# Block-masked attention and a feed-forward layer: the first product of scores takes 128 rows instead of 68

## The chip, the cores and the metric

The kernel runs on one core of a Trainium2 chip. The metric is the time of one execution on the device, in microseconds (us). The core has five engines with queues of their own: PE (TensorE, the matrix unit), DVE (VectorE), ACT (ScalarE), POOL (GpSimd) and SP (SyncE, which here issues every DMA transfer). A matmul is two instructions on PE: a load of the stationary operand (LDWEIGHTS, shown as the lane PEld) and the MATMUL itself, which streams the moving operand past it.

## The reference

Eight batches of eight heads, 576 positions, 64 numbers per head; q, k and v are random. Each position sees its own block of 64 positions and all blocks before it. What comes out of the attention, 4608 rows of 512, goes through two matrices with a nonlinearity between them.

```python
scores = scale * np.matmul(q, k.transpose(0, 1, 3, 2))
mask = block_i >= block_j                     # blocks of 64 positions
scores = np.where(mask, scores, -1000000000.0)
scores = scores - np.max(scores, axis=-1, keepdims=True)
attn = np.exp(scores)
attn = attn / (np.sum(attn, axis=-1, keepdims=True) + 1e-09)
out = np.matmul(attn, v)
...
h = x @ w_in                                  # 4608x512 @ 512x2048
g = np.where(h >= 1, h, np.where(h <= -1, 0.0, (h + 1) ** 2 / 4))
return g @ w_out                              # 4608x2048 @ 2048x512
```

## The kernel before

**Two streams of work share the engines.** The attention goes pair by pair (two heads at a time; 8 batches of 4 pairs). The feed-forward layer goes by chunks of 512 rows and 128 hidden columns: `ffn_in` (L806, twelve matmuls of 512 columns) and `ffn_out` (L830 and L835, twelve more). Both are written as generators of steps and interleaved; the feed-forward layer follows the attention at a distance of one chunk.

**Numbers in two parts.** Most matmuls read the 32-bit type fp32r, which keeps fewer digits; so an operand is split in a high part and a low part (the rounding error of the high part), and a product is the sum of high by high, high by low and low by high.

**The scores.** In batches 0 and 1 the scores are plain 32-bit products of 64 rows (L555), and the mask is added by a small product of the tile `hide` (L563). `hide` is 128 rows by 2 by 64 columns; it is zero but for its rows 0 and 64. From batch 2 on (`far` and `raw` pairs) the method `product` makes them by two matmuls that accumulate in one bank `ps_s`:

- L531 multiplies `qa` and `ka`. Rows 0 to 63 of these tiles hold the high parts of q and k, one row for each of the 64 numbers of a head; rows 64 to 67 hold four rows of a mask (`mrow`), put there once at the start by the DMAs of L251 and L252. So the matmul takes KA = 64 + 4 = 68 rows. Rows 68 to 127 of both tiles are neither written nor read.
- L532 multiplies `qb` and `kb`, 128 rows, which carry high by low and low by high at once.

A pair has two heads and four tiles of 128 queries each, with 128, 256, 384 and 512 keys: eight such products a pair, 24 pairs, 192 in all. The last 64 queries of both heads go another way (`scores_last`, L609 and L612). Then come the softmax (DVE and ACT), a round trip by DMA that turns the weights into fp32r (`prr<-pr`), their transposes on PE (L636) and the product with v (L687). For each later pair, the DMAs of L477 copy the high parts from `qb` and `kb` into rows 0 to 63 of `qa` and `ka`.

**The order on each engine is fixed.** After all instructions are emitted, the tables `QUEUES` (one for each engine, compressed) tell in which order they stand in that engine's queue. They were made for one list of instructions: a kernel that emits other instructions needs other tables. PE, DVE and ACT take their queue strictly in turn, and so does SP, which issues the DMAs. The landings of SP's DMAs are counted by eight semaphores in rotation (they are named DMAHW0 to DMAHW7); before a DMA is issued, the one eight places ahead of it must have landed.

**Names on the way:** `qn`, `kn` and `en` are q, k and their last blocks as loaded for batches 0 and 1; `qk` holds them transposed; `bits` is a piece of a weight matrix that is being split, `ws` and `wo_split` the split pieces of w_out on chip and in memory, `wo` a piece loaded again; `xl` and `spare` take the round trip of the weights in batch 1.

Of the kernel before, what the change touches and what calls it, by code (L numbers as in the profile page):

```python
# [11 lines left out]
F32 = mybir.dt.float32  # L12
# [61 lines left out]

QUEUES = {
    "PE": (
        'c-rk&S#ld85CsNik!)F3BrA(ksY)d|g%9D|<OVrIZkL}NB)tL6Ald#;zgM$}VW9i*nvruoybEq{k?x1miY*DwgS6o<M+ZM0R'
        'A1*NdKNqCS@ad>L@dBQ9_+JmmoUJ4L1qqW{5+m>e}Q`-<Bz)qP88oY==|GQ*HQV4PqH4ds8jXR*uwFf?q+GZrq-_}uGG!;Q{'
        'H|H>IgahD63c3?^&+1yAk4wj>14>JOOK5BedjR+83=iUW#mx^MN?ZtaU8L{t6#}N9l7<JQZ!<0jokYa8sUf)R;jk>eiJ#LL{'
        's{9{1$Yh5R;Av}2P6wq>27dxY~RBIAAGdbO)Z+xf@F&9x0HVoQ;1;J_70QVYHItXvSD$a#)(otnDJvm~X8_GR_$wo!8Is+LE'  # L80
        '(qbzRSj;d}4zxQ;9?6G!zC^}4(ftUTri=H19tF|v=fhcw>jXh;N!ZC~gaz)e~?~<$M5@U_}K<?x`7Fw5CRnZK(RpJV6XfK**'
        '_3nTNc+bmQxy~jUEqk-yb*9cW{SKCKLq3o64vsTW-_P*tQAYki)J{cB&#&mZo)6zjqFy3pQ>pD<{k2EieYDm+#~!G%0y#f(Q'
        '10O~kL2MQW)(?Sj*%75xlJ@y{(@A_LLMcnp6EJ~BXVm{UjzTDPC@#&wOke9>|&XnJrc_Mv58X8>?KoQGUl9J(KM?yHa^sjoX'
        'OQuc9Oa~4aMuYnhQCJxu|cpm-#%^KJyYzUDflxrN7|l_^;ynFYcS{NgTsj{CIY61AYmxE`PxJJGJm0)PHaB{{)VX89X#m_WL'
        'QXUQoMcD!L<&z<j@JRwYVbWTLsWat4FJU@#aA27|$1Fc=I5gTY`h7z_r3!C){L3<kshf`9Kz7zY'
    ),
    "DVE": (
        'c-rk$+fKtU3_VGjrfV5!0>m3a3<UrGg*cv@#7SEO4@_e7QKC8*AKy}7gaK$c1Prh^Nz@(95qCWA(c^}ON$3fIzXmz)=%y13m'
        'aWY8z$`mPCwg4jvz0@-4bmo>M`U>-lycw|Lv|k72E?Kl&b)Hs$hHR>fxjLY*;DYjxN^@vfa4Av7n0R@|5mh#c8(mA#S8B~^I'
        '0qQf-t=@mc)v8?=-*BII1|1;)vQOo&6xR;t8duWv<4={-UY|B&t})o@?vnR?pDh+T>HG?36MxG`C}WyFznVmUeH}W8d5oI$<'  # L90
        'A+elb{=iMvVL>{WD55LZU29ID-Xy05;GGByxg1r(VApFk7)QZ7sdT>-ChKWD@hwcpA};Fr^Kq3Alz7vFcs{Tx#5w;0-vIr(X'
        'eSX#FEweBd6A+1Ed?4fCHXtq%8X*N^rS!K~krRx53%H!qS)H60S*;RGV@nMy#y>HUL)hym}$#X9`%>Ns07n?ofi{8UVboJ?O'
        'p?i(We_KVr61(|Ehx~O>Fs;kExpd9`S8Ugs{haS_qq{t|>wCMtx68@n?|9BFUxp_LiU'
    ),
    "Activation": (
        'c-rk!?Q+8)46{r~((a?()^&UTC!H~lgURx*cfIZgmjoP3mIXvagUm7#Edw$K*|SGynj}_p6CE^Xv~1Shi~c|A`z+5yuf}!M@'
# [6 lines left out]
        'c-muNzzrC&@EPH3Mg}G*%>tyE!E6?&8i*<;6xA@j$SN4I+Qx`s^GF8(GI#(c'  # L103
    ),
    "SP": (
        'c-rk#yKWRg5Uifv+uhr{UEdw}d3X4Y2oXXA{sbffzQK;{%&{L55kf)&$&zydLWCSy;sXdsAs`|k;UfsBuAMu91=s-+iKn&mt'
        'gi0rnN5+RB}-8PXv1h3EkS`d+6U)}W(m)a5paZ>sDdY5yhG02oaSC8Y)MQH9U_dFjAtG81;<*<Eq*<IhBX|rZxeL`=k&{kS|'
        'sWP<9Tdg4m0#~#0(ASqhcQv9m+eAd9*+?oZ&=%vovts!9eJ~vaXd?o3o6)XOk<VK&~L(H0Eg0+qt~u%-TIG`DW5wipBF@mDV'
        'isO%NtFh-+PAG0ncBo;=pSC7wcfkK#K)c(1}8>1x!KteQuf=<wYI+>W&ly00N_#q3l0xb?*p$lH_J5%;<gRq$-U3J2ES*ZX7'
        'u=J6aKv^KowxW{oeY5^lSTc!B{v+_!uVvF3lPF}_sH<kG}BD+yT73*nI+QXRrmQ|6tz(@A?Y=ul`%GZdP)7z@$H}N0f3%<)I'  # L110
        'U_(0(xVUeR*_ZgllOcA^SUvD|64hx{_iW1SE0*w#pXto>#!au-$Gev34Lr1wZqV;<lQl`OZD~{j91`WL&sKBo3O8Blw-ywss'
        'l311NA^@@EBT&YnNOeCj;&)^Oy0(N#g5%z6tL1=Dl~p$GJ;x$T)j4%-azA*#vAfK<X7|k6&Vz#QSm#^`3rW@GoN}kkta-lk3'
        'Et>dH*@~zxBM<d#(5X>J5?iGDN`7EydN^RdG%G0gmoAg8'
    ),
}

# [7 lines left out]
def block_attn_then_ffn(  # L124
# [232 lines left out]
    class Pair:  # L357
# [27 lines left out]
        def load_qk(self):
            if not self.raw:
                self.load("q")
                self.load("k")
# [4 lines left out]
            for i, src in enumerate(copies):
                for j in range(2):
                    head = src[self.b, 2 * self.hp + j]
                    nc.sync.dma_start(
                        self.qk[:, j * NTL : (j + 1) * NTL, i, :].bitcast(F32),
                        head[:SM].rearrange("(p t) d -> p t d", t=NTL),  # L400
                    )
# [126 lines left out]
            self.pb = att1.tile([P, 2, NTL, G1], F32, tag=f"pb{turn}", name=f"pb{turn}")  # L528

        def product(self, ps, j, c0, n):  # L530
            nc.tensor.matmul(ps, qa[:KA, j, c0 : c0 + P], ka[:KA, j, :n], start=True, stop=False)  # L531
            nc.tensor.matmul(ps, qb[:, j, c0 : c0 + P], kb[:, j, :n], start=False, stop=True)  # L532

        def inverse(self, total):
# [399 lines left out]
```

## Time and profile before

| | |
|---|---|
| time before, median of 3 runs | 1170.87 us (1169.71 to 1171.76) |
| the profiled execution's own time | 1173.48 us |
| its span, first to last instruction | 1171.4 us |
| mean granted clock of TensorE | 0.996 |
| PE busy | 1140.3 us, 97% of the span |
| DVE, ACT, POOL busy | 716.0, 623.7, 268.3 us |
| mean busy share of the DMA queue's transfers | 61.2% of 16 engines |

How to read the rows. A group's row has the line, the engine, the operation, `out<-in`, the number of rows and columns of the stationary operand in use (`68*128`), the shape of the moving operand, the count, the busy time in us with the mean duration of one in ns, and the idle time ahead of them. Matmuls overlap: one of 512 columns is shown with 389 to 400 ns although a new one starts each 0.23 us, so a sum of durations is not time. A row of the timeline has the start, the time it took, the engine and the instruction. PEld and PE are two lanes of the same engine.

### The profile page before, as it was taken

How to read it: one execution, taken by the hardware profiler on the slowest of the kernel's cores; microseconds unless marked ns; L12 is line 12 of the kernel's file. 1: busy time of each engine (PE TensorE's matmuls, PEld its weight loads, DVE VectorE, ACT ScalarE, POOL GpSimd, SP SyncE). 2: the span in 40 equal slices, each digit the busy share in tenths (PEclk: the TensorE clock that was granted, in tenths of full speed). 3: DMA queues.
4: the chain of work that ended last, by engine and by line, in shares of the span. 5: the costliest groups of instructions: out<-in, count | busy, mean ns of one | idle time of the engine just before them, and what ended most of it. 6: DMA issues, size and time to landing. Idle time of an engine off the chain costs nothing.

```text
span 1171.4 us, 19270 instructions
## 1 busy us (share of the span) xinstructions
PE 1140.3 (97%) x6384; PEld 905.8 (77%) x6384; DVE 716.0 (61%) x1858; ACT 623.7 (53%) x1531; POOL 268.3 (23%) x215
## 2 busy tenths in 40 slices
PE   7889998999999999999999999999999999999998
PEld 4556666778888888888888888888888888888886
DVE  7887887666666666666666666666666663222222
ACT  6887766455555555555555555555555553222222
POOL 3443555111121121111111111111111112222222
PEclk9999999999999999999999999999999999999999
DMA  6778777687887876665556565665566443423423
GB/s 190 226 231 245 261 231 235 189 240 235 246 263 237 256 230 187 174 202 180 169 163 212 177 177 172 201 187 173 165 206 196 132 146 98 140 90 96 138 90 108
DMA packets 195649, 219.54 MB, mean 187 GB/s; under 512 B 131280, under 2 KB 145616, under 8 KB 194784
## 3 DMA queue, kind: packets, MB, share of 16 engines
q1 hardware_dynamic: 195552, 218.33, 61.2%
q8 instruction: 51, 0.84, 0.3%
q14 instruction: 46, 0.38, 0.1%
HBM read 135.79 MB, written 31.98 MB: 143 GB/s over the span
## 4 chain that ended last, share of the span: by engine, by line
PE 83%; DVE 1%; DMA 1%; ACT 0%; issue 0%; POOL 0%; SPq 0%; ACTq 0%
PE ph L806 32%; PE po L830 21%; PE po L835 10%; PE ps_av L687 6%; PE ps_t L636 4%; PE ps_s L531 4%; PE ps_s L532 3%; PE ps_qk L469 1%; PE ps_s L609 1%; PE ps_s L612 1%; DMA wo<-wo_split 0%; DMA qn<-in_q_dram 0%; DVE t L816 0%; DVE t L819 0%; PE ps_s L555 0%
## 5 line engine op out<-in xcount | busy, mean ns | idle before, releaser
L821 POOL TENSOR_TENSOR gl<-t,gh 128x512 fp32r<-128x512 f32 x144 | 188.9, 1312 | 804.1 <-ACT gh L820 700.9
L830 PE MATMUL po<-wo,gh 128*128 128x512 f32 x1152 | 304.0, 397 | 0.9 <-DMA wo<-wo_split 0.5
L830 PEld LDWEIGHTS po<-wo,gh 128*128 128x128 f32 x1152 | 212.9, 189 | 45.5 <-ACT ps_s L583 0.7
L806 PE MATMUL ph<-xh,wih 128*128 128x512 f32 x576 | 230.1, 400 | 2.1 <-DVE t L819 2.1
L806 PE MATMUL ph<-xh,wil 128*128 128x512 f32 x576 | 227.2, 394 | 0.0
L806 PE MATMUL ph<-xl,wih 128*128 128x512 f32 x576 | 226.2, 393 | 0.0
L816 DVE SCALAR_TENSOR_TENSOR t<-t 128x512 f32<-128x512 f32 x144 | 101.5, 705 | 189.6 <-ACT t L815 189.5
L815 ACT ACTIVATE t<-ph 128x512 f32<-128x512 f32 x144 | 86.2, 599 | 176.0 <-PE ph L806 175.8
L835 PE MATMUL po<-wo,gl 128*128 128x512 f32 x576 | 164.0, 393 | 0.2 <-POOL gl L821 0.2
L820 ACT CAST gh<-t 128x512 fp32r<-128x512 f32 x144 | 89.3, 620 | 111.5 <-DVE t L819 111.4
L583 ACT ACTIVATE pr<-ps_s,nm 128x128 f32<-128x128 f32 x192 | 100.4, 525 | 82.7 <-DVE nm L578 68.5
L578 DVE TENSOR_REDUCE nm<-ps_s 128x1 f32<-128x384 f32 (+3 forms) x256 | 121.4, 485 | 25.6 <-PE ps_s L532 12.6
L835 PEld LDWEIGHTS po<-wo,gl 128*128 128x128 f32 x576 | 108.3, 188 | 23.6 <-POOL gl L821 0.6
L806 PEld LDWEIGHTS ph<-xh,wih 128*128 128x128 f32 x576 | 108.3, 188 | 23.2 <-DVE t L819 2.6
L806 PEld LDWEIGHTS ph<-xh,wil 128*128 128x128 f32 x576 | 108.2, 188 | 23.0
L806 PEld LDWEIGHTS ph<-xl,wih 128*128 128x128 f32 x576 | 108.4, 188 | 19.3 <-DVE xl L697 0.2
L819 DVE TENSOR_TENSOR t<-ph,t 128x512 f32<-128x512 f32 x144 | 98.8, 686 | 2.3
L636 PEld LDWEIGHTS ps_t<-ident_r,prr 128*128 128x128 f32 x600 | 68.6, 139 | 21.5 <-issue 0.4
L537 DVE TENSOR_SCALAR sm<-sm 128x1 f32<-128x1 f32 x256 | 37.2, 151 | 77.1 <-ACT pr L583 69.2
L651 ACT COPY pb<-ps_t 128x512 f32<-128x512 f32 (+1 forms) x128 | 68.0, 532 | 10.3 <-PE ps_t L636 8.3
L589 DVE TENSOR_SCALAR pr<-pr,sm 128x128 f32<-128x128 f32 (+2 forms) x192 | 70.0, 385 | 4.6 <-DVE sm L538 0.3
L636 PE MATMUL ps_t<-ident_r,prr 128*128 128x128 f32 x600 | 70.7, 236 | 0.0
(95 smaller groups left out, 1442.9 us busy)
## 6 DMA issues: line engine op xcount, KB each, us to landing
wo<-wo_split SPq DMA_DIRECT2D x144, 512.0 KB, 3.6
prr<-pr SPq DMA_DIRECT2D x96, 192.0 KB, 2.7
prr<-pr SPq DMA_DIRECT2D x48, 256.0 KB, 2.6
out_dram<-ob SPq DMA_DIRECT2D x36, 256.0 KB, 3.7
bits<-in_moe_w_in_dram SPq DMA_DIRECT2D x16, 512.0 KB, 4.4
vs<-in_v_dram SPq DMA_DIRECT2D x64, 128.0 KB, 3.5
bits<-in_moe_w_out_dram SPq DMA_DIRECT2D x16, 512.0 KB, 4.0
wo_split<-ws SPq DMA_DIRECT2D x16, 512.0 KB, 3.2
```

What stands on the lines that cost most here:

```text
L578: nc.vector.tensor_reduce(out=nm[:, i : i + 1], in_=ps[:, cs], axis=AX.X, op=ALU.max, negate=True)
L583: nc.scalar.activation(raw[:, cs], ps[:, cs], AF.Exp, bias=nm[:, i : i + 1], scale=1.0, accum_out=sm[:, i : i + 1],)
L636: nc.tensor.transpose(out.bitcast(F32R), src, ident_r)
L687: nc.tensor.matmul(ps[j * D : (j + 1) * D, lo_col:], self.vs[j][:, kt, :], x, start=i == 0, stop=i == len(heads[0]) - 1,)
L806: nc.tensor.matmul(ph, w[:, cc, fs], x[:, cc, xs], start=(cc == 0 and i == 0), stop=(cc == NCC - 1 and i == 2),)
L815: nc.scalar.activation(t_, ph, AF.Relu, bias=0.5, scale=0.5)
L816: nc.vector.scalar_tensor_tensor(out=t_, in0=t_, scalar=1.0, in1=t_, op0=ALU.min, op1=ALU.mult)
L819: nc.vector.tensor_tensor(out=t_, in0=ph, in1=t_, op=ALU.max)
L820: nc.scalar.copy(gh, t_)
L821: nc.gpsimd.tensor_tensor(out=gl, in0=t_, in1=gh.bitcast(F32), op=ALU.subtract)
L830: nc.tensor.matmul(po[tt], gh[:, ts_], wo[:, w, :], start=(fc == 0 and w == 0), stop=False)
L835: nc.tensor.matmul(po[tt], gl[:, ts_], wo[:, 0, :], start=False, stop=fc == NFC - 1)
```

## The change

Three things are done.

- The first matmul of `product` takes all 128 rows of `qa` and `ka`, not the first 68.
- So that rows 68 to 127 add nothing, a new method `clear_below` fills them with zeros, once, by two DMAs (one for `qa`, one for `ka`; 60 rows of 8 pieces of 512 bytes, 240 KB each). They read `hide`, whose rows 4 to 63 are zero, and they read the same 128 columns eight times. They are emitted when q and k of the first pair of batch 2 are fetched.
- The tables of PE, DVE and SP are new, since two more instructions are emitted.

```diff
 QUEUES = {
     "PE": (
-        'c-rk&S#ld85CsNik!)F3BrA(ksY)d|g%9D|<OVrIZkL}NB)tL6Ald#;zgM$}VW9i*nvruoybEq{k?x1miY*DwgS6o<M+ZM0R'
...
+        'c-rk&+i}}45IleYNlBJ$E0UFmGnvUGslr9Ln{<#G(p`R1NbZFfLD~M#?G8y11cAH79w>kw4m=DHs(S*p$T9GJfQaX)eTLjFn'
...
         def fetch(self):
             if self.raw:
+                if (self.b, self.hp) == (RAW, 0):
+                    self.clear_below()
                 for dst, src in zip(copies, (q, k)):
...
+        def clear_below(self):
+
+            part, _, cols = hide[KA - D : D, :, :].ap
+            zeros = bass.AP(
+                tensor=hide.tensor, offset=hide[KA - D : D, :, :].offset,
+                ap=[part, [0, 2 * SM // P], [1, P]],
+            )
+            for t_ in (qa, ka):
+                nc.sync.dma_start(
+                    t_[KA:].bitcast(F32).rearrange("p j (n c) -> p (j n) c", c=P), zeros
+                )
...
         def product(self, ps, j, c0, n):
-            nc.tensor.matmul(ps, qa[:KA, j, c0 : c0 + P], ka[:KA, j, :n], start=True, stop=False)
+            nc.tensor.matmul(ps, qa[:, j, c0 : c0 + P], ka[:, j, :n], start=True, stop=False)
             nc.tensor.matmul(ps, qb[:, j, c0 : c0 + P], kb[:, j, :n], start=False, stop=True)
```

The new lines push later ones down: L531 becomes L545, L555 becomes L569, L563 becomes L577, L823 becomes L837.

The first place is on SP, in the work of batch 1, where the two new DMAs stand. Names ahead of the bracket are as above; in the bracket are the semaphores that the row waits for (the numbers behind the underscore say nothing). Before:

```order
L436 DMA kn<-in_k_dram 128x4x64 [waits DMAHW4_49,PE_49]
L823 DMA wo<-wo_split 128x1024 [waits DMAHW6_49,DMAHW5_49,PE_49]
L347 DMA xl<-pr 128x384 [waits DVE_49]
L315 DMA wo_split<-ws 128x1024 [waits DMAHW7_49,Pool_49]
L436 DMA qn<-in_q_dram 128x4x64 [waits DMAHW0_49]
L347 DMA xl<-pr 128x384 [waits DMAHW1_49,DVE_49]
L266 DMA bits<-in_moe_w_in_dram 128x1024 [waits DMAHW2_49]
L436 DMA qn<-in_q_dram 128x4x64 [waits DMAHW3_49]
L315 DMA wo_split<-ws 128x1024 [waits DMAHW4_49,Pool_49]
L347 DMA xl<-pr 128x384 [waits DMAHW5_49,DVE_49]
```

and now:

```order
L450 DMA kn<-in_k_dram 128x4x64 [waits DMAHW4_49,PE_49]
L395 DMA qa<-hide 60x8x128 [waits DMAHW5_49]
L395 DMA ka<-hide 60x8x128 [waits DMAHW6_49]
L837 DMA wo<-wo_split 128x1024 [waits DMAHW7_49,PE_49]
L347 DMA xl<-pr 128x384 [waits DMAHW0_49,DVE_49]
L315 DMA wo_split<-ws 128x1024 [waits DMAHW1_49,Pool_49]
L450 DMA qn<-in_q_dram 128x4x64 [waits DMAHW2_49]
L347 DMA xl<-pr 128x384 [waits DMAHW3_49,DVE_49]
L266 DMA bits<-in_moe_w_in_dram 128x1024 [waits DMAHW4_49]
L450 DMA qn<-in_q_dram 128x4x64 [waits DMAHW5_49]
L315 DMA wo_split<-ws 128x1024 [waits DMAHW6_49,Pool_49]
L347 DMA xl<-pr 128x384 [waits DMAHW7_49,DVE_49]
```

The two stand behind `kn` and ahead of `wo`. The eight rows behind them each wait for another landing than before; from the last row shown on, every row waits for the same transfer as before (the last `xl` waits for this `wo` in both). No other row of SP moved, and nothing else on it was added.

The second place is on PE, in the first pair of batch 0, where plain scores (of `qk`) and their mask (of `hide`) are made. Before:

```order
L555 MATMUL ps_s<-qk_145 64x64
L555 MATMUL ps_s<-qk_145 64x128
L563 MATMUL ps_s<-hide 64x64 x2
L555 MATMUL ps_s<-qk_145 64x192
L555 MATMUL ps_s<-qk_145 64x256
L563 MATMUL ps_s<-hide 64x64
```

and now:

```order
L569 MATMUL ps_s<-qk_145 64x64
L569 MATMUL ps_s<-qk_145 64x128
L577 MATMUL ps_s<-hide 64x64
L569 MATMUL ps_s<-qk_145 64x192
L577 MATMUL ps_s<-hide 64x64
L569 MATMUL ps_s<-qk_145 64x256
L577 MATMUL ps_s<-hide 64x64
```

One small matmul of the mask stands one row later. Seventeen rows of PE moved in this manner, all in batches 0 and 1 and nearly all of L563, by one place or two. From batch 2 on, the rows of PE stand as they stood, and no product of scores waits for a semaphore that it did not wait for before.

The third place is on DVE, at the start of the program, where `hide` is filled and the first q and k are taken out of `ps_qk`. Before, two fills of `hide` stood ahead of the copy into `qk`:

```order
L512 TENSOR_SCALAR qc_108<-ps_qk 64x64 x2
L248 MEMSET hide 1x64 x2
L513 COPY qk_145<-ps_qk 128x64
L273 TENSOR_SCALAR bits<-bits 128x512
L578 TENSOR_REDUCE nm<-ps_s 128x1 x2
```

and now they stand behind it:

```order
L526 TENSOR_SCALAR qc_108<-ps_qk 64x64 x2
L527 COPY qk_145<-ps_qk 128x64
L248 MEMSET hide 1x64 x2
L273 TENSOR_SCALAR bits<-bits 128x512
L592 TENSOR_REDUCE nm<-ps_s 128x1 x2
```

Two other small fills of DVE moved by a place. ACT and POOL stand as before.

More of the change, by code (lines that the diff above doesn't have):

```diff
@@ L76 @@
     "PE": (
-        'c-rk&S#ld85CsNik!)F3BrA(ksY)d|g%9D|<OVrIZkL}NB)tL6Ald#;zgM$}VW9i*nvruoybEq{k?x1miY*DwgS6o<M+ZM0R'
[L78 to L85, printed above, removed]
+        'c-rk&+i}}45IleYNlBJ$E0UFmGnvUGslr9Ln{<#G(p`R1NbZFfLD~M#?G8y11cAH79w>kw4m=DHs(S*p$T9GJfQaX)eTLjFn'
@@ new lines @@
+        'D|-f2#ZnE)#<T8_VLh@Ev#X{SUq0l2;Jxaf01`c!5`QoCywtLmib@n<utPOxMYM-wY2vDJ3M~#uUT8Jsr73S*D|)B`u1B;Mo'
+        '7_zyn0^yJnMCa8zrsisPw8i;R%`Iiueq2ui6)_H(rV?^*%C3owbZ5xVyp!<VpM7GtXJucgUj9jNImD5;bKIv!lz(o-h(opN@'
+        'O>=!VsrIOeg*g4&W!0Uq)Ei79xWxm@ky(RTi^st%~ys3LY8iRWxQM(%kfdhOHd3eW63;9RGsuF|T;N|oA|#kadg$+4?i8R?d'
+        'z-ot^b?tu4uy#w}Ci>2#*)?wld9OpzWqUXnoMcbFL!PyThy99YRVkT0z$%o_!`L*WiImcL{KC(L{kFqwYie}WUkXCTZd(p(J'
+        'cZ)pYdoHi2)Y-(NC2#h-&eXX^DiT(z?uLCH_#GN&;J%;n?omhnz^t80nqFSfbvYls6;-{+%0^XmSW$oJQCN8*ex%qvSC&V0x'
@@ L86 @@
+        '0yrb9y!ZM4xdq0fpwL=PZUqNO+411SrpDn86~M6`8u*AQme1N2JTgzy!LNvxhNvpg*>}>#OL=z6J<TK(@b5?SaOD}X;N!!d{'
+        '{ejW>*K@Ny_e2z7DjS8+MX#Q+>0Y&gZ!Hg=;u>RWJKi{RJn-e^u9ifp5AeNembD;|1OZ`VvrG{=oBhZrL;Y?=AhGpwTIVhbG'
+        'E?Kb6(<)vg({?!*%^{XR6S60|Qd>h4~YGZ+j8gTY`h7z_r3!C){L3<iV2U@#aA27|$1Fc|(9`~#@R7wr'
     ),
     "DVE": (
-        'c-rk$+fKtU3_VGjrfV5!0>m3a3<UrGg*cv@#7SEO4@_e7QKC8*AKy}7gaK$c1Prh^Nz@(95qCWA(c^}ON$3fIzXmz)=%y13m'
-        'aWY8z$`mPCwg4jvz0@-4bmo>M`U>-lycw|Lv|k72E?Kl&b)Hs$hHR>fxjLY*;DYjxN^@vfa4Av7n0R@|5mh#c8(mA#S8B~^I'
@@ L90 @@
[L90 to L93, printed above, removed]
+        'c-rk$+fKtU3_VHOrWdwp0>m3a3<UrGg*cv@#7SEO4@_e7QQA5eAKy}7gaK$c46x{MmY@e%`Z~}s*wNY@4HMB3Jb(3Ze}h>pT'
@@ new lines @@
+        'd`3OECZtvJ<ROb%27@S=`hiAM3N^$E=Qg*Wap7>KrFVxnP$!$$#ze}^Vb6-c?#YaX71SsaNM5bLbMvr??szv<-{>ryzuHX@3'
+        'msj3)3rONvwGHPR}<QClv=`96|e}y&r^HT0*XAaq^znUli4VL>21Tacx^U)iJcUHu}^kJGqPu&F$FUkZBIfQm@T==$k#E5%w'
+        '|b7lU<~xSO=iPDSSgVP=%dp;%43yW$%$V?DtYK$a=+4pgx(<-!!u6=+rN=Zv_l_FEb8d~<3pWL>BE!u@WzpM9+T7DL@JXFqK'
+        'gOU*Xl)`8;a<4oX79-8WeX7k0GDgH)j%_@sVDpmHMQywqprhH;ElTA_g6dzW(>hmW4Tg~Dr7d>w!hv|Q#?P9ZM+N}4m5nZ{v'
+        'S?FG)@?Tf6U5VX%qeK3>$e7mU(p<V`|0}jz&3?}Jx6xf6+wH#H?%Va`@pn9zmM_1J2#x'
@@ L105 @@
     "SP": (
[L106 to L113, printed above, removed]
+        'c-rk#yKWRg5Uifv+uhsSUEdw}0e1&}B8Lbe0)GOM1AhZVkP(A;L<orh0>}x7EktC=u>+?jAR=($k8nVB?c5109uAO5JguE)b'
+        '#+(IY>E^eS&9-s7e>oy2@33LADkzeB|LwQfM;lkDtJ<1A31k(ntPeBB{6;Uh%jO@p7q!l92+rr`1Sc2R`Ha5m#9nFqhBu66{'
+        '6lUp2r3jFh@T}%+Y`WYW6|Vp}Z5BM+-E=XS|c&JPlm;Fcf;AtQ%$3<t$_G+2qP7kSmBcjX7HM2A1euDVv;`yLT=BOu9=kdG0'
+        'IHn?=qk!o&#it!XS~3TkS~;~jLwQwZ--d?yI+mDrTFR$<A?d8DZp-(A9uSnr@a8{t}1kjlqxAf`axz7&tSS4C98vmvV-Sbtw'
+        'XA_K69*ErPLaKP~)$N8uQjNojw=8u_`SK>Xk$erutO^k6_nV%3@MGZCY2jX$1eN5PISsj@R9I?M;%Vhebe2s_&y{|@oQ~x2p'
+        ';Z!~W>)N@)#ckVRU*Zc-MtESx>VdbDs7@=oYg1;&xQbW&OlPKdZhFZ+-n2yT;I55zgMNP-tVx1<mPRGO6QX?e)f%o{;RY+cY'
+        'eA9P%KOXRwwEef$v5@EeEP!f+ZwKm$=gIP*|F=40#>@BLgP0fBdBG>)km}04YYn~ydnQfem37<mO*h^6~FRaJY#1)^O<KGdC'
+        'K(X*kc)#_wQr>Th9x<7kdA%-Vk~Jh6wnvr8r+ZFRpFh0q3bUuK'
     ),
```

## The prediction

> **What bounds the kernel now.** I read the page first, then PE's groups by shape, then single rows of the timeline. The page:
>
> ```profile
> span 1171.4 us, 19270 instructions
> PE 1140.3 (97%) x6384; PEld 905.8 (77%) x6384; DVE 716.0 (61%) x1858; ACT 623.7 (53%) x1531; POOL 268.3 (23%) x215
> ```
>
> PE is the bound; it idles 31 us in all. The table by stages tells where: in the columns stand the length, the busy time of PE, PEld, DVE, ACT and POOL with counts, the granted clock, the share of DMA and GB/s.
>
> ```profile
> 30.00:60.00 30.00, 26.92 (x197) 16.34 (x198) 26.80 (x86) 26.86 (x71) 11.88 (x10) 0.94 0.74 219
> 180.00:200.00 20.00, 17.99 (x113) 12.66 (x112) 15.16 (x37) 13.15 (x31) 13.85 (x10) 0.92 0.76 252
> 260.00:600.00 340.00, 339.76 (x1944) 276.65 (x1943) 221.25 (x590) 188.71 (x482) 56.68 (x43) 1.00 0.71 215
> ```
>
> From 260 us on PE is idle for 0.24 us in 340: there a nanosecond more or less of PE is a nanosecond of the whole. Before 200 us, in batches 0 and 1, PE has gaps. The 192 changed matmuls lie in the saturated stretch:
>
> ```profile
> L531 PE MATMUL ps_s<-ka,qa x192: 223/336/498, 217.8 to 970.3; 68*128 68x128 f32 x48, 68*128 68x256 f32 x48, 68*128 68x384 f32 x48, 68*128 68x512 f32 x48
> ```
>
> So the question is whether such a matmul costs PE less time with 128 rows. The groups by shape seem to say yes:
>
> ```profile
> L531 PE MATMUL ps_s<-ka,qa 68*128 68x512 f32 x48 | 22.7, 473 | 0.2 <-DVE qc L506 0.2
> L531 PE MATMUL ps_s<-ka,qa 68*128 68x384 f32 x48 | 19.5, 406 | 0.0
> L532 PE MATMUL ps_s<-kb,qb 128*128 128x512 f32 x48 | 18.9, 395 | 0.0
> L532 PE MATMUL ps_s<-kb,qb 128*128 128x384 f32 x48 | 16.3, 340 | 0.0
> L531 PE MATMUL ps_s<-ka,qa 68*128 68x256 f32 x48 | 15.9, 332 | 0.0
> L531 PE MATMUL ps_s<-ka,qa 68*128 68x128 f32 x48 | 13.8, 288 | 0.0
> L532 PE MATMUL ps_s<-kb,qb 128*128 128x256 f32 x48 | 13.6, 283 | 0.0
> L532 PE MATMUL ps_s<-kb,qb 128*128 128x128 f32 x48 | 13.1, 273 | 0.0
> ```
>
> Size for size the 68-row matmul lasts longer by 78, 66, 49 and 15 ns, together 208 ns, and 48 x 208 ns = 10.0 us. Were the rows the cause, the change would bring 10 us. But the two groups differ in a second thing: L531 stands first, behind short matmuls or a switch of tile, and L532 stands behind L531.
>
> **The rows or the place.** A long 128-row matmul that stands behind short ones is needed for comparison. The feed-forward layer has them: at 501 us a first L806 of 512 columns stands behind four transposes. Of each row I take the start (first number, us); the start of the next matmul is when PE is free again.
>
> ```profile
> 501.67 0.19 PEld L806 LDWEIGHTS ph<-xh,wih 128*128 128x128 f32 x1
> 501.71 0.47 PE L806 MATMUL ph<-xh,wih 128*128 128x512 f32 x1
> ...
> 502.01 0.39 PE L806 MATMUL ph<-xl,wih 128*128 128x512 f32 x1
> ...
> 502.24 0.39 PE L806 MATMUL ph<-xh,wil 128*128 128x512 f32 x1
> ```
>
> This 128-row matmul is shown with 470 ns too, and holds PE for 0.30 us where its successor holds it for 0.23. From the start of its weight load (501.67) to the next matmul (502.01) are 0.34 us. Now the 68-row one of 512 columns, behind transposes, and another behind the product with v:
>
> ```profile
> 529.37 0.19 PEld L531 LDWEIGHTS ps_s<-ka,qa 68*128 68x128 f32 x1
> 529.41 0.46 PE L531 MATMUL ps_s<-ka,qa 68*128 68x512 f32 x1
> ...
> 529.71 0.40 PE L532 MATMUL ps_s<-kb,qb 128*128 128x512 f32 x1
> ...
> 514.57 0.19 PEld L531 LDWEIGHTS ps_s<-ka,qa 68*128 68x128 f32 x1
> 514.58 0.50 PE L531 MATMUL ps_s<-ka,qa 68*128 68x512 f32 x1
> ...
> 514.91 0.39 PE L532 MATMUL ps_s<-kb,qb 128*128 128x512 f32 x1
> ```
>
> 529.71 - 529.37 = 0.34 and 514.91 - 514.57 = 0.34 us: the same as with 128 rows. The MATMUL's record begins before its weights are in, so the extra 70 to 100 ns is the wait for its own load, which was begun late because what stood ahead was short. That load takes as long for 68 rows as for 128 (0.19 us in all these rows).
>
> The 256-column matmul stands behind no transpose but behind a 128-column L532, which is short as well:
>
> ```profile
> 504.82 0.19 PEld L532 LDWEIGHTS ps_s<-kb,qb 128*128 128x128 f32 x1
> ...
> 504.94 0.19 PEld L531 LDWEIGHTS ps_s<-ka,qa 68*128 68x128 f32 x1
> 504.99 0.33 PE L531 MATMUL ps_s<-ka,qa 68*128 68x256 f32 x1
> ...
> 505.17 0.28 PE L532 MATMUL ps_s<-kb,qb 128*128 128x256 f32 x1
> ```
>
> Expected for 128 rows: 0.34 us less the streaming of 256 columns, 395 - 283 = 112 ns by the groups above, so 0.23 us. Found: 505.17 - 504.94 = 0.23 us. For 128 columns the partner itself serves: L532's load at 504.82 to the next matmul at 504.99 is 0.17 us, and I expect that of a 128-row first matmul. So the four sizes show no cost of 68 rows.
>
> **The change part by part.**
>
> *192 matmuls with 128 rows.* 0 ns each. The rows are rounded to 0.01 us, and a difference of two of them can hide 0.01 us: 192 x 0.01 = 1.9 us either way. I take 0 and keep both ends.
>
> The Trainium skill has a rule that could give the groups' reading a cause: its page TensorEngine Tiling (Array Packing), section Key Properties, says that a change of tiling mode drains the array. Its table of configurations knows row tiles of 128, 64 and 32, and 68 rows fit only the first, so by that page no mode changes between L531 and L532. If they did count as two modes, the drains would vanish with the change and the sum would be that of the 10 us. The trace speaks for no switch, 0.23 us found against 0.23 expected.
>
> *Two transfers.* Issued by SP behind `kn`:
>
> ```profile
> 142.84 0.59 SPq L436 DMA_DIRECT2D kn<-in_k_dram  x1
> 148.37 0.33 SPq L823 DMA_DIRECT2D wo<-wo_split  x1
> ```
>
> SP idles from 143.43 to 148.37, 4.9 us; two issues at about 0.6 us each, as that of `kn`, end near 144.7. The transfers move 480 KB. The DMA engines in the stretch 143 to 149 us, tenths of busy share in slices of 0.15 us:
>
> ```profile
> DMA  9999999579789699999963211100000000000000
> ```
>
> and, of the list of DMA issues by line, like transfers with their KB and the us to landing:
>
> ```profile
> qa<-qb SPq DMA_DIRECT2D x48, 128.0 KB, 3.9
> ...
> spare<-pr SPq DMA_DIRECT2D x12, 256.0 KB, 3.1
> ```
>
> The engines run empty from about 146.3 us to the end of that stretch. At the 281 GB/s of the next busy stretch,
>
> ```profile
> 150.00:160.00 10.00, 9.53 (x70) 6.12 (x69) 8.31 (x18) 6.57 (x16) 5.69 (x5) 1.00 0.83 281
> ```
>
> 480 KB are 1.7 us of DMA, and the hole holds them. They land by about 148.6 (144.7 + 3.9). The rows of SP that now wait for them are the `qn` and `wo_split` further down, issued before at 153.44 and 156.62 us: 5 us to spare. The first reader is the product at 217.8 us. Price 0; if the cover were gone, if `wo` and the rows behind it landed later by all of this in a stretch where PE waits, it is 1.7 us.
>
> *Moved rows.* PE's 17 rows lie before 203 us. The query on the tile `hide` has what DVE waited for L563 over the whole program (us, times), and the fills:
>
> ```profile
> L248 DVE MEMSET hide<- x2: 112/112/112, 8.0 to 8.2; 1x64 f32 x2
> ...
>   DVE nm L578: 11.5, 9
> ```
>
> and the list of PE's waits has one of that time at the start:
>
> ```profile
> PE ps_s L555 <- DVE qk L513: 1.0, 1, 1.0
> ```
>
> A mask product that stands one row later ends some tenths of a us later; nine of them had DVE waiting, and PE has gaps there. I bound it by 1 us of delay and take 0. On DVE the copy of L513 comes forward by two fills, up to 0.3 us of gain, while the first L563 waits for these fills instead; I take 0.
>
> Sum: 0, with bounds -1.9 and -0.3 below, +1.9, +1.7 and +1.0 above. The profiled execution took 1173.48 us (span 1171.4 and 2.1 around it), 2.6 more than the median of the runs; a change of 0 is 1173.5 of that, and **1170.9 us** on the scale of the median.
>
> **The rivals.**
>
> *The rows do cost* (10.0 us faster, 1160.9). For it: the groups' means, the same sign in all four sizes. Against it: the three pairs of rows above, and that 128-row matmuls behind short ones carry the same 470 ns. Chance 0.06.
>
> *A small gain in batches 0 and 1* (about 3 us faster, 1168). The table by stages shows the clock at 0.94 in 30 to 60 us and 0.92 in 180 to 200: 30 x 0.06 = 1.8 and 20 x 0.08 = 1.6 us of full clock lost, each after PE had idled. If moved rows close the gap that set off one of them, that 1.7 comes back, and with the gap itself and the 0.3 of the fills it passes 2.3 us. Against it: the moved rows are single ones of 0.2 us. Chance 0.06.
>
> *The zeros are in the way* (about 3 us slower, 1174). Mechanism: the two transfers are slow, so that `wo` and the round trips `xl<-pr` behind them land late, PE idles in 150 to 200 us, and the clock falls once more. Price: 1.7 us of DMA passed on to PE, and 1.7 of clock, 3.4 in all. It decides from the point at which the transfers land later than about 151 us, over 6 us behind their issue; the rows of like transfers show 3.1 and 3.9. Chance 0.10.
>
> On the clock, the Trainium skill (TensorE: Matmul & The Clock Gate, Part 1: The HAM clock gate) tells of a gate that halves the clock for a window of 3.4 us after one idle window; half of that is 1.7 us, which agrees with the 1.6 and 1.8 of the rows.
>
> *The zeros are not needed or not used* can't be: without them the rows below 67 hold whatever the memory held, and the matmul reads them.
>
> **How the numbers follow.** The forecast has 0.78, and its time is 1170.9. A measurement of this kernel can't tell less than about 0.2%, 2.3 us, from no change. Faster: 0.06 + 0.06 = 0.12. Slower: 0.10. The range: the bounds of the matmuls and of the moved rows, -2.2 below and +2.9 above, and 0.7 more below for the scatter of the runs (1169.7 to 1171.8), so 1168.0 to 1173.8. It leaves out the first rival and the larger half of the others.
>
> **What would show it.** Right: the first matmul's groups now read 128*128 with means near 473, 406, 332 and 288 ns, unchanged, and PE's busy time stays near 1140 us; from the load of a 512-column one to the next matmul stay 0.34 us; the zeros are issued near 144 us and land by 149, and PE's waits before 200 us are as they were. Wrong: means of 395, 340, 283 and 273 and some 10 us less of PE (the rows cost after all); or `wo` and `xl` landing late at 150 us, or a third stretch with a clock under 1.00.

## The result: the change made the kernel slower, by some 0.25 to 0.5%

| | median (lowest to highest), us | kernel before beside it, us | ratio to before [95%] |
|---|---|---|---|
| the changed kernel | 1177.18 (1175.12 to 1180.12), 5 runs | 1171.52 (1169.71 to 1172.60), 5 runs | 1.0054 [1.0034, 1.0073] |
| the same kernel, measured again beside the experiments | 1175.56 (1172.53 to 1179.44), 11 runs | 1172.99, 34 runs | 1.0025 [1.0011, 1.0039] |

The ratios, and the means further down, leave out four executions of 1.4 to 6.3 ms in one of the later groups. The prediction was 1170.9 us and no change, with a range to 1173.8. Both ratios lie above the 0.2% within which I called two times the same, and both intervals exclude 1. The profiled execution took 1178.68 us. Its page gives a span of 1176.6 us, so the span grew by 1176.6 - 1171.4 = 5.2 us. The row of the changed matmul's line (count; ns least, median, most; first and last start) tells on which side of it they lie:

```profile
L545 PE MATMUL ps_s<-ka,qa x192: 220/334/498, 222.2 to 975.3; 128*128 128x128 f32 x48, 128*128 128x256 f32 x48, 128*128 128x384 f32 x48, 128*128 128x512 f32 x48
```

Before, these 192 matmuls ran from 217.8 to 970.3. So 4.4 of the 5.2 us are lost ahead of the first of them, in batches 0 and 1, where no matmul has new rows; from the first to the last lie 753.1 us, before 752.5, so 0.6 more. The groups by shape:

```profile
L545 PE MATMUL ps_s<-ka,qa 128*128 128x512 f32 x48 | 22.8, 475 | 0.2 <-DVE qc L520 0.2
L545 PE MATMUL ps_s<-ka,qa 128*128 128x384 f32 x48 | 19.4, 404 | 0.0
L545 PE MATMUL ps_s<-ka,qa 128*128 128x256 f32 x48 | 15.9, 331 | 0.0
L545 PE MATMUL ps_s<-ka,qa 128*128 128x128 f32 x48 | 13.7, 286 | 0.0
```

Means of 475, 404, 331 and 286 ns, with 68 rows 473, 406, 332 and 288: a first matmul of 128 rows costs what one of 68 rows costs.

**The zeros.** SP's rows (start, time, and what it issues) and the list of DMA issues (KB, us to landing) of the changed kernel:

```profile
145.62 0.59 SPq L450 DMA_DIRECT2D kn<-in_k_dram  x1
146.26 1.05 SPq L395 DMA_DIRECT2D qa<-hide  x1
147.37 0.93 SPq L395 DMA_DIRECT2D ka<-hide  x1
151.11 0.33 SPq L837 DMA_DIRECT2D wo<-wo_split  x1
```

```profile
qa<-hide SPq DMA_DIRECT2D x1, 240.0 KB, 6.5
ka<-hide SPq DMA_DIRECT2D x1, 240.0 KB, 6.8
```

Issued at 146.26 and 147.37, they landed near 152.8 and 154.2: later than I had worked out. Yet `wo`, the next row of SP, was issued at 151.11, 5.5 us behind `kn` as before (142.84 and 148.37), and each of the seven rows behind `wo` stands as far behind `kn` as before, to within some 0.2 us.

**Where in batches 0 and 1.** In the rest of this text "the third pair's stretch" is the time from the third pair's first scores of 320 columns to the next pair's first scores of 64 columns. Rows of the timeline of the kernel before, with start, time, engine and, in brackets, what the engine waited for:

```profile
51.55 0.87 PE L555 MATMUL ps_s<-qk 64*64 64x320 f32 x6
...
54.80 0.68 DVE L578 TENSOR_REDUCE nm<-ps_s 128x1 f32<-128x512 f32 x1
...
57.60 0.42 DVE L273 TENSOR_SCALAR bits<-bits 128x512 f32<-128x512 f32 x1
57.80 1.38 POOL L289 TENSOR_TENSOR wil<-bits,wih 128x512 fp32r<-128x512 f32 x1 [1.74 <-ACT wih L287]
...
60.95 0.33 PE L555 MATMUL ps_s<-qk 64*64 64x64 f32 x3
```

and of the changed kernel:

```profile
49.35 0.87 PE L569 MATMUL ps_s<-qk 64*64 64x320 f32 x6
...
50.77 0.56 DVE L592 TENSOR_REDUCE nm<-ps_s 128x1 f32<-128x384 f32 x1 [0.35 <-PE ps_s L577]
...
53.29 0.69 DVE L592 TENSOR_REDUCE nm<-ps_s 128x1 f32<-128x512 f32 x1 [0.20 <-PE ps_s L577]
...
56.03 1.30 POOL L289 TENSOR_TENSOR wil<-bits,wih 128x512 fp32r<-128x512 f32 x1 [1.76 <-ACT wih L287]
56.10 1.52 DVE L273 TENSOR_SCALAR bits<-bits 128x512 f32<-128x512 f32 x1
...
60.55 0.33 PE L569 MATMUL ps_s<-qk 64*64 64x64 f32 x3
```

Before it takes 60.95 - 51.55 = 9.40 us, after 60.55 - 49.35 = 11.20. Two things make up the 1.80. First, the maxima of the scores (L592) now wait for mask products (L577), and by the third maximum DVE is 53.29 - 49.35 = 3.94 us into the stretch, where it was 54.80 - 51.55 = 3.25: 0.7 late. Second, DVE's L273, a piece of the splitting of a weight matrix, lasts 1.52 us, not 0.42: 1.1 more. Before, it began 0.20 us ahead of POOL's L289; now, 0.7 us late on its side, it begins 0.07 us behind it, and ends 0.29 us after it.

The Trainium skill (SBUF — State Buffer, section Who interferes with whom) has a rule for such a meeting: DVE, in certain kinds of operation, and GpSimd share a pair of ports of the on-chip memory; the operation that starts first holds it to its end, and the other is blocked until then. The trace agrees in the main: the one that starts first keeps its length (0.42 for DVE, 1.30 for POOL), and DVE, when second, ends just behind POOL. When POOL is second it is blocked for less than the rule says: 1.38 against 1.30, though DVE went on for 0.22 us of it.

There is a third loss in this profiled execution. Stages of it, in the columns of the table by stages (length, busy time of PE, PEld, DVE, ACT, POOL, granted clock, DMA share, GB/s):

```profile
102.50:105.80 3.30, 2.72 (x21) 1.61 (x21) 0.45 (x3) 1.22 (x3) 1.96 (x2) 0.97 0.69 240
105.80:112.60 6.80, 6.80 (x25) 4.95 (x26) 4.41 (x16) 4.96 (x15) 4.05 (x3) 0.51 0.75 215
```

For 6.8 us the clock was halved, with PE busy throughout. Whether that comes of the change, and what it costs, is a question for the experiments.

### The profile page after: what moved, and what is told of

It reads as the page before. It is cut to its first block, busy times and chain, and to the rows that moved or that the text cites. A ratio compares the mean times of both kernels' runs of the same rounds, so it can differ in the third digit from the quotient of the medians.

```text
span 1176.6 us, 19272 instructions
## 1 busy us (share of the span) xinstructions
PE 1144.4 (97%) x6384; PEld 904.7 (77%) x6384; DVE 718.0 (61%) x1858; ACT 622.9 (53%) x1531; POOL 267.5 (23%) x215
## 4 chain that ended last, share of the span: by engine, by line
PE 87%; DVE 6%; ACT 3%; issue 1%; DMA 1%; SPq 1%; POOL 0%; ACTq 0%; DVEq 0%
PE ph L820 32%; PE po L844 21%; PE po L849 11%; PE ps_av L701 7%; PE ps_t L650 4%; PE ps_s L545 4%; PE ps_s L546 3%; PE ps_s L569 1%; PE ps_qk L483 1%; PE ps_s L623 1%; DVE nm L592 1%; DVE bits L279 1%; PE ps_t L652 1%; DVE bits L273 1%; DVE pr L603 1%
## 5 line engine op out<-in xcount | busy, mean ns | idle before, releaser
L820 PE MATMUL ph<-xh,wih 128*128 128x512 f32 x576 | 230.8, 401 | 2.0 <-DVE t L833 2.0
L820 PE MATMUL ph<-xh,wil 128*128 128x512 f32 x576 | 227.8, 395 | 0.0
L820 PE MATMUL ph<-xl,wih 128*128 128x512 f32 x576 | 227.0, 394 | 0.0
L592 DVE TENSOR_REDUCE nm<-ps_s 128x1 f32<-128x384 f32 (+3 forms) x256 | 121.1, 484 | 27.1 <-PE ps_s L577 12.9
L820 PEld LDWEIGHTS ph<-xh,wih 128*128 128x128 f32 x576 | 108.5, 188 | 23.6 <-DVE t L833 2.5
L820 PEld LDWEIGHTS ph<-xh,wil 128*128 128x128 f32 x576 | 108.3, 188 | 23.2
L820 PEld LDWEIGHTS ph<-xl,wih 128*128 128x128 f32 x576 | 108.5, 188 | 19.9 <-DVE xl L711 0.2
```

The lines of the kernel that those rows point to most:

```text
L592: nc.vector.tensor_reduce(out=nm[:, i : i + 1], in_=ps[:, cs], axis=AX.X, op=ALU.max, negate=True)
L820: nc.tensor.matmul(ph, w[:, cc, fs], x[:, cc, xs], start=(cc == 0 and i == 0), stop=(cc == NCC - 1 and i == 2),)
```

## The experiments

Theories: **T1**, the moved rows of batches 0 and 1 cost the time (the third pair's stretch above all). **T2**, the two transfers do. **T3**, 128 rows do. The texts that were written ahead of the runs call them A, B and C. The kernels ran in three groups, each on one chip with the kernel before beside it.

### The changed kernel again

No edit.

> The changed kernel once more, beside the others on the same chip. All theories: 1.003 to 1.007 of the kernel before. In the profile PE should have fallen 4 to 5 us behind the kernel before by 200 us and keep that distance to the end within 1 us, and each 68-row matmul's successor with 128 rows should again show 473 to 475 ns at 512 columns.

1175.56 us, ratio 1.0025 [1.0011, 1.0039]; the stretch is 11.20 us again, and the 192 matmuls run from 219.7 to 973.0. The loss repeats, at half its first size and just under the range expected. This execution has its halved clock elsewhere (10.2 us of it from 14 us on, 3.4 from 198 on) and none at 106: where that happens differs between executions of one kernel.

### The moved rows alone

The kernel before with the new order of PE and DVE; 68 rows, no zeros, SP as before.

```diff
-QUEUES PE, DVE: before
+QUEUES PE, DVE: the order of the changed kernel
 product: qa[:KA, ...], ka[:KA, ...]      # 68 rows
 no clear_below
```

> The kernel before (68 rows, no zeros), with the changed kernel's order of rows on PE and DVE. Theory A (the moved rows of batches 0 and 1 make the loss): 1.003 to 1.007. Theory B (the two transfers of zeros make it) and theory C (128 rows make it, about 1 us, in the saturated stretch): 0.998 to 1.002.

1176.07 us, ratio 1.0026 [1.0015, 1.0036], beside 1.0025 of the whole change in the same group. The timeline has the same meeting:

```profile
51.11 0.87 PE L555 MATMUL ps_s<-qk 64*64 64x320 f32 x6
...
57.79 1.30 POOL L289 TENSOR_TENSOR wil<-bits,wih 128x512 fp32r<-128x512 f32 x1 [1.75 <-ACT wih L287]
57.86 1.52 DVE L273 TENSOR_SCALAR bits<-bits 128x512 f32<-128x512 f32 x1
...
62.31 0.33 PE L555 MATMUL ps_s<-qk 64*64 64x64 f32 x3
```

62.31 - 51.11 = 11.20 us. The ratio lies just under what T1 was expected to give and above what T2 and T3 allow here. T1 holds: the moved rows reproduce the loss with neither zeros nor 128 rows.

### The zeros alone, and the zeros with 128 rows

Both keep PE's and DVE's order of before, and SP's of the changed kernel.

```diff
 QUEUES PE, DVE: before
+clear_below()                             # the two transfers
 product: qa[:KA, ...], ka[:KA, ...]       # first kernel: 68 rows
-product: qa[:KA, ...], ka[:KA, ...]
+product: qa[:, ...], ka[:, ...]           # second kernel: 128 rows
```

> The two transfers of zeros at their place on SP, but the matmul stays at 68 rows and PE and DVE keep the order of the kernel before. Theory B: 1.003 to 1.007. Theories A and C: 0.998 to 1.002.

> The transfers of zeros and the 128 rows, with the order of PE and DVE of the kernel before: the change without its moved rows. Theory A: 0.998 to 1.002. Theory B: 1.003 to 1.007. Theory C: about 1.001, that is 1 us more than the run with zeros and 68 rows.

1172.78 us, ratio 0.9998 [0.9984, 1.0013], and 1173.15 us, ratio 0.9998 [0.9984, 1.0012]. The stretch is 9.40 in both. T2 and T3 fall: neither zeros nor rows change the time by as much as the loss. The second kernel also had 6.8 us of halved clock near 105 us in its profiled execution, with PE's order of before; so that window in the changed kernel does not need the moved rows.

The rows of the changed line and one of the rows of the feed-forward layer (from 230 to 970 us), with 68 rows:

```profile
L545 PE MATMUL ps_s<-ka,qa x192: 223/336/506, 215.9 to 968.1; 68*128 68x128 f32 x48, 68*128 68x256 f32 x48, 68*128 68x384 f32 x48, 68*128 68x512 f32 x48
...
L820 PE MATMUL ph<-xl,wih x376: 387/389/398, 231.8 to 967.3; 128*128 128x512 f32 x188
```

and with 128:

```profile
L545 PE MATMUL ps_s<-ka,qa x192: 220/334/503, 218.2 to 971.3; 128*128 128x128 f32 x48, 128*128 128x256 f32 x48, 128*128 128x384 f32 x48, 128*128 128x512 f32 x48
...
L820 PE MATMUL ph<-xl,wih x376: 389/393/402, 229.8 to 969.8; 128*128 128x512 f32 x188
```

From first to last 752.2 us with 68 rows and 753.1 with 128. That 0.9 us lies not in L545 (median 334 against 336 ns), but other matmuls, of which L820 (389 to 393 ns) is the clearest, are shown longer by some ns. Durations overlap, so starts are the better measure. Between the first and the last of the 192, the time from each L820 to the start of the next matmul, all added up, is 268.1 us with 68 rows and 269.5 with 128; for L545 and L546 together it is 71.2 and 70.9. So L820 becomes dearer by 1.4 us, the changed products cheaper by 0.3, and the rest of the difference is spread over other lines.

### 96 rows

```diff
-product: qa[:, ...], ka[:, ...]
+product: qa[:96, ...], ka[:96, ...]
```

The order of PE and DVE as before, with the zeros.

> Zeros, and 96 rows in the first product, with the order of PE and DVE of the kernel before. From the first to the last of the changed matmuls passed 752.1 to 752.5 us with 68 rows and 753.1 to 753.3 with 128. Theory C1 (each row more costs): about 752.6. Theory C2 (only the full array behaves differently): 752.3 or 753.2, one of the two. If 128 rows saved anything in these matmuls, 96 would save a part of it; no theory that is left expects that.

1169.57 us, a single run, inside the scatter of the kernel before.

The 192 matmuls run from 214.1 to 966.2, 752.1 us from first to last: with 96 rows the 0.9 us is absent, and the sum over L820 is 268.1 us. It belongs to the full 128 (753.1, 753.3, 753.1 and 753.4 in four traces, against 752.1 to 752.6 in all of fewer rows). What it is was not found; against the totals it is too small to be seen.

### Two rows alone, twice

Of all moved rows only two, on PE in the third pair.

```diff
 L555 MATMUL ps_s<-qk_568 64x384
-L563 MATMUL ps_s<-hide 64x64
-L638 MATMUL ps_t<-ident_r,pr 128x128 x3
+L638 MATMUL ps_t<-ident_r,pr 128x128
+L563 MATMUL ps_s<-hide 64x64
+L638 MATMUL ps_t<-ident_r,pr 128x128 x2
...
 L555 MATMUL ps_s<-qk_568 64x512
-L563 MATMUL ps_s<-hide 64x64
-L638 MATMUL ps_t<-ident_r,pr 128x128 x3
+L638 MATMUL ps_t<-ident_r,pr 128x128
+L563 MATMUL ps_s<-hide 64x64
+L638 MATMUL ps_t<-ident_r,pr 128x128 x2
```

> The kernel before with two rows of PE moved: in the third pair of batch 0 two mask products (L563) stand behind one transpose instead of ahead of it. Theory A (late mask products delay the softmax on DVE, and a fill of DVE, L273, then meets a subtraction of POOL and lasts 1.5 instead of 0.4 us): from the third pair's first scores of 320 columns to the fourth pair's first scores of 64 columns 11.20 us as in the changed kernel, not 9.40 as before, and about 1.0015. Rival (the loss is spread over many moved rows, these two are nothing): 9.40 us and 1.000.

> The kernel with the two moved mask products once more, to narrow its time, which was 1.0000 of the kernel before with an interval of 0.9985 to 1.0015 although its third pair was 1.8 us later. Theory A1 (the 1.8 us reach the end): 1.0010 to 1.0020. Theory A2 (they are made good behind the third pair): 0.999 to 1.0005. In both the stretch of the third pair is 11.20 us.

In the third pair these two do the whole of it: the first maximum waits 0.37 us for L563, and

```profile
49.75 0.87 PE L555 MATMUL ps_s<-qk 64*64 64x320 f32 x6
...
56.42 1.31 POOL L289 TENSOR_TENSOR wil<-bits,wih 128x512 fp32r<-128x512 f32 x1 [1.75 <-ACT wih L287]
56.50 1.52 DVE L273 TENSOR_SCALAR bits<-bits 128x512 f32<-128x512 f32 x1
...
60.95 0.33 PE L555 MATMUL ps_s<-qk 64*64 64x64 f32 x3
```

the stretch is 60.95 - 49.75 = 11.20 us, in the second trace 11.20 too. The totals are less plain: 1174.06 us with ratio 1.0000 [0.9985, 1.0015], then 1174.11 us with 1.0011 [1.0000, 1.0023]. The 1.8 us would be 1.0015, the upper end of the first interval and inside the second; a mean of the two ratios is 1.0005. By the means of the runs the two rows cost 1.0 us (1173.68 against 1172.70) and 1.6 us (1174.12 against 1172.50). So the local loss is shown, and how much of it reaches the end is not.

### All moved rows but these two, twice

```diff
-QUEUES PE, DVE: before
+QUEUES PE, DVE: the order of the changed kernel, but the two rows above left where they were
```

> All moved rows of PE and DVE but these two, without zeros, with 68 rows. Theory A: 9.40 us in that stretch, and 1.001 (the 3.0 us of all moved rows less the 1.8 of the two). Rival: 11.20 us or near, and 1.0026.

> All moved rows but these two once more. Theory A1: 1.0005 to 1.0012. Theory A2 (the other moved rows make the loss): 1.002 to 1.003. In both the stretch of the third pair is 9.40 us.

```profile
51.46 0.87 PE L555 MATMUL ps_s<-qk 64*64 64x320 f32 x6
...
57.52 0.42 DVE L273 TENSOR_SCALAR bits<-bits 128x512 f32<-128x512 f32 x1
57.72 1.37 POOL L289 TENSOR_TENSOR wil<-bits,wih 128x512 fp32r<-128x512 f32 x1 [1.74 <-ACT wih L287]
...
60.86 0.33 PE L555 MATMUL ps_s<-qk 64*64 64x64 f32 x3
...
104.27 0.34 PE L555 MATMUL ps_s<-qk 64*64 64x64 f32 x5 [0.98 <-DVE qk L513]
...
138.76 0.32 PE L555 MATMUL ps_s<-qk 64*64 64x64 f32 x2
```

The stretch is back at 9.40 us, with DVE's L273 ahead of POOL and 0.42 us long. But a second place shows: from the scores that begin at 104.27 us to those at 138.76 are 34.49 us. The kernel before:

```profile
104.05 0.34 PE L555 MATMUL ps_s<-qk 64*64 64x64 f32 x5 [0.98 <-DVE qk L513]
...
137.84 0.33 PE L555 MATMUL ps_s<-qk 64*64 64x64 f32 x2
```

33.79 us, so the other moved rows cost 0.70 here. DVE's rows tell by what. First the kernel before, then all but the two:

```profile
118.28 1.02 DVE L578 TENSOR_REDUCE nm<-ps_s 128x1 f32<-128x384 f32 x2 [0.45 <-PE ps_s L563]
...
118.74 1.02 DVE L578 TENSOR_REDUCE nm<-ps_s 128x1 f32<-128x384 f32 x2 [0.71 <-PE ps_s L563]
...
123.06 1.29 DVE L578 TENSOR_REDUCE nm<-ps_s 128x1 f32<-128x512 f32 x2 [0.63 <-PE ps_s L563]
```

The first maxima wait 0.26 us longer for mask products, and the next two, which waited for nothing before, wait 0.63: 0.89 together, of which 0.70 are left at 138 us. No operation of DVE or POOL lasts longer here: this place is waits for mask products alone. By traces:

| kernel | third pair's stretch, us | near 104 to near 138 us, us | ratio |
|---|---|---|---|
| before | 9.40 | 33.79 | |
| zeros alone | 9.40 | 33.74 | 0.9998 |
| two rows alone | 11.20 | 34.15 | 1.0000, 1.0011 |
| all but the two | 9.40 | 34.49 | 1.0008, 1.0008 |
| moved rows alone | 11.20 | 34.48 | 1.0026 |
| changed kernel again | 11.20 | 34.50 | 1.0025 |

Four traces had 6.8 us of halved clock inside the second stretch and stand apart: 37.53 us in the changed kernel's first trace, 37.55 in the second one of all but the two, 36.81 with the zeros and 128 rows, 36.80 in the second one of the two rows. The moved rows cost 0.7 here too. The two rows cost nothing in it, so their 34.15 in the table isn't a loss that repeats. And the halved clock costs 3.0 us (37.53 against 34.50): with the two places, more than the 4.4 us by which the 192 matmuls began later in the first profiled execution. The kernel before has halved clock too, 3.4 us from 33 and 3.4 from 197, so the three don't add up exactly.

The totals were 1173.57 us, ratio 1.0008 [0.9991, 1.0025], and 1174.35 us, ratio 1.0008 [0.9993, 1.0022]. The two places add to 1.80 + 0.70 = 2.5 us, 0.21% of 1173, against 0.25 and 0.26% measured. The halves (0.05 and 0.08%) add to less, within their intervals. By the means of the runs all but the two cost 1.2 us (1173.85 against 1172.70) and 1.3 us (1173.76 against 1172.50); with the 1.0 and 1.6 of the two rows that makes 2.1 to 2.9 us, near the 3.2 of all moved rows by the same measure (1175.87 against 1172.69). How the loss splits between them stays open.

### The changed kernel with one row of DVE later

DVE's L273 goes behind the three small rows that follow it, so that it no longer begins during POOL's L289.

```diff
 L551 TENSOR_SCALAR sm<-sm 128x1
-L273 TENSOR_SCALAR bits<-bits 128x512
 L552 RECIPROCAL sm<-sm 128x1
 L592 TENSOR_REDUCE nm<-ps_s 128x1
 L603 TENSOR_SCALAR pr<-ps_s,sm 128x512
+L273 TENSOR_SCALAR bits<-bits 128x512
```

> The changed kernel with one row of DVE moved: L273 stands three places later, behind a reciprocal, a maximum and a scaling that the attention waits for. Theory A with the meeting of DVE and POOL as its larger part: L273 lasts 0.42 us again, the stretch falls from 11.20 to about 10.1 us, and the kernel by 1.1 us, to about 1.0015 of the kernel before. Rival (L273 was long because its data came late, or POOL has nothing to do with it): L273 stays at 1.5 us or another row takes its place, and the stretch stays at 11.2.

```profile
49.43 0.87 PE L569 MATMUL ps_s<-qk 64*64 64x320 f32 x6
...
56.10 1.30 POOL L289 TENSOR_TENSOR wil<-bits,wih 128x512 fp32r<-128x512 f32 x1 [1.75 <-ACT wih L287]
56.37 0.67 DVE L592 TENSOR_REDUCE nm<-ps_s 128x1 f32<-128x512 f32 x1
57.62 0.42 DVE L273 TENSOR_SCALAR bits<-bits 128x512 f32<-128x512 f32 x1
...
59.32 0.33 PE L569 MATMUL ps_s<-qk 64*64 64x64 f32 x3
```

L273 lasts 0.42 us again and the stretch 59.32 - 49.43 = 9.89 us. So the later place of this row is worth 11.20 - 9.89 = 1.31 us. That is more than the 1.10 by which the meeting had made L273 longer: L273's own 0.42 us no longer stands ahead of rows that the attention waits for, and how much of the 1.31 that is was not measured apart. 0.49 us of the 1.80 remain. L592, which reads a bank of products and begins inside POOL's operation, keeps its 0.67 us: not every operation of DVE is held up. The total, 1175.17 us with ratio 1.0021 [1.0004, 1.0039], lies 0.04 points below that of the changed kernel in another group, less than the interval, so the gain at the end isn't shown.

### The kernel before with four rows of DVE later

Such meetings stand in the kernel before too. Here four of the DVE rows are put later; nothing else differs.

```diff
@@ near 18 us
-L276 TENSOR_SCALAR shifted<-bits 128x512
 L578 TENSOR_REDUCE nm<-ps_s 128x1
 L589 TENSOR_SCALAR pr<-ps_s,sm 128x384
+L276 TENSOR_SCALAR shifted<-bits 128x512
@@ near 98 us: L276 two rows later, near 168 us: L276 one row later
@@ near 191 us
-L273 TENSOR_SCALAR bits<-bits 128x512
 L697 TENSOR_TENSOR xl<-ps_av,xh 128x256
+L273 TENSOR_SCALAR bits<-bits 128x512
```

> The kernel before, with four weight-splitting rows of DVE (L276 at 18, 98 and 168 us, L273 at 191 us) that met a POOL instruction and lasted 0.8 to 1.6 us put one or two places later, behind maxima and scalings that the attention waits for. If such meetings hold the attention up: these rows last 0.42 us, and the kernel is up to 2 us faster, 0.998 to 0.9995. Rival (the meetings move to other rows, or the splitting itself is what is late): 1.000 to 1.001.

The four rows in the trace:

```profile
19.12 0.50 DVE L276 TENSOR_SCALAR shifted<-bits 128x512 uint32<-128x512 uint32 x1
...
96.94 0.43 DVE L276 TENSOR_SCALAR shifted<-bits 128x512 uint32<-128x512 uint32 x1
...
165.09 1.28 DVE L276 TENSOR_SCALAR shifted<-bits 128x512 uint32<-128x512 uint32 x1
...
188.94 0.42 DVE L273 TENSOR_SCALAR bits<-bits 128x512 f32<-128x512 f32 x1
```

They lasted 1.56, 0.90, 1.52 and 0.82 us in the kernel before: together 4.80, now 2.63. The third still begins inside an operation of POOL (164.79 to 166.09) and keeps 1.28 us. The kernel takes 1170.95 us against 1172.36 beside it, ratio 0.9985 [0.9975, 0.9996]. The interval excludes 1, so it is the fastest kernel of this study, by about 1.4 us; the 0.2% that I had named as the least that can be told lies above that.

## Why the prediction was wrong

**Rows or place: right.** The prediction read the longer first matmul as one that waits for its own weight load, and priced 128 rows at 0 within 1.9 us. All four means stayed, and the zeros with 128 rows give 0.9998 [0.9984, 1.0012]. The 0.9 us that 128 rows do cost lies inside the bound, but in other matmuls than the bound spoke of. The rival *the rows do cost* is ruled out. That the first matmul waits for its own load rests on the prediction's rows; no run moved that load.

**The two transfers: right price, wrong landing.** Taken as 0, measured 0.9998 [0.9984, 1.0013]. I had them land by 148.6 with 3.9 us each, from rows of other transfers. (Two issues of 0.6 us behind 143.43 end at 144.6, not at 144.7; in the run they took 1.05 and 0.93.) They took 6.5 and 6.8 us, and landed past the 151 us, over 6 us behind their issue, from which my rival *the zeros are in the way* was to decide. With the zeros alone they took 6.1 and 6.6 us, over the mark as well. It did not decide: nothing had become later by them that was waited for. So the direction of that rival came true, and nearly its size (3.4 us priced, 3 measured), by luck: the mechanism was another.

**The moved rows: the step that failed.** The prediction said "I bound it by 1 us of delay and take 0". The mechanism was named, a mask product that stands later makes DVE wait, but the term was mis-sized: alone it measures 1.0026 [1.0015, 1.0036], 3 us, of which 2.5 are seen in the traces at two places. The bound counted the waits themselves, some tenths of a us for each moved row. Already these pass it: 0.7 us at the third pair and 0.70 near 120 us. What it did not count at all is the next row behind them: 0.7 us late on DVE is enough to change who starts first, DVE's L273 or POOL's L289, and DVE, now the second, waits out the other's operation, 1.1 us. A query of DVE's and POOL's rows in that stretch would have shown the two 0.20 us apart. And the stage was one in which DVE had little to spare: the prediction's own row for 30 to 60 us shows DVE busy 26.80 us, PE 26.92.

The rival *a small gain in batches 0 and 1* looked at the same rows with the other sign and is ruled out with it. The front part's "seventeen rows" on PE compares rows by name; matmuls that read alike hide five more. By the tables of order it is twenty-two.

**The measurement.** I gave the scatter of the runs 0.7 us. The kernel before alone spans 1168.24 to 1175.85 us in the second measurement. Is the loss only halved clock, which differs from run to run? In the second measurement the mean granted clock of the runs is 0.994 for the kernel before, 0.996 for the changed kernel and 0.995 for the moved rows alone, so the slower kernels had no less of the clock. In the first five runs of the changed kernel it goes from 0.992 (1180.12 us) to 0.999 (1175.26), and even that last run is 3.7 us above the median before. What repeats with the moved rows is 1.0025. Whether the rest of the first 1.0054 is the clock, the chip, or chance in five runs, is open.

## What to carry to other kernels

Where two more instructions force a new order by hand, the order can cost more than the instructions: time the new order with the old work (one kernel) before blaming the new work. A delay of some tenths of a us is not bounded by itself where two engines that hold each other up run close together: list the pairs of long operations on DVE and POOL that begin within the delay of each other, and price an exchange at the length of the other's operation. And a longer mean duration of the first instruction in a chain says where it stands, before it says what it is.

## What the runs showed of the hardware that I had not expected

**A start 0.01 us earlier decides who waits.** Near 180 us the kernel before starts another part of the splitting on DVE and POOL's L289 in one and the same hundredth of a us:

```profile
180.63 0.69 DVE L279 SCALAR_TENSOR_TENSOR bits<-bits,shifted 128x512 uint32<-128x512 uint32 x1
...
180.63 1.84 POOL L289 TENSOR_TENSOR ws<-bits,ws 128x512 fp32r<-128x512 f32 x1 [0.78 <-DVE shifted L276]
```

and the kernel with four rows later:

```profile
177.09 1.86 DVE L279 SCALAR_TENSOR_TENSOR bits<-bits,shifted 128x512 uint32<-128x512 uint32 x1
...
177.08 1.30 POOL L289 TENSOR_TENSOR ws<-bits,ws 128x512 fp32r<-128x512 f32 x1 [0.77 <-DMA bits<-in_moe_w_out_dram]
```

In the trace's own ns DVE is 2 ns ahead in the first kernel, and POOL 12 ns ahead in the second. Whoever is first keeps its length (0.69 or 1.30 us) and the other takes 1.84 or 1.86: 0.5 us more for POOL, 1.2 for DVE. The faster kernel has the worse outcome for DVE here, so not all of its 2.17 us on the four rows is a gain of DVE's.

**The halved clock does not need a long idle stretch.** In the changed kernel it set in near 105.6 us, behind 3.3 us in which PE was busy for 2.72 and the longest idle gap was 1.00 us, and lasted 6.8 us; other executions have it elsewhere. The Trainium skill (TensorE: Matmul & The Clock Gate, Part 1: The HAM clock gate) tells of windows of 3.4 us, which agrees with 6.8 as two of them, and puts the halving down to an idle window; no idle window of that length stands there.

**128 rows cost the matmuls around them.** 0.9 us in 752: L820, which did not change, becomes dearer by 1.4 us, other lines cheaper by 0.5. With 96 rows it is absent. The cause is open.
